# Attention plus gated feed-forward on one core: query weights loaded by halves of 512 columns and 512 rows, and a new order for every engine

## The chip, the cores and the metric

The kernel runs on 1 core of one Trainium2 chip. The metric is the device time of one execution in microseconds (us). Engines are named as in the profile: PE (matmul), PEld (its weight loads), DVE (vector), ACT (activation), POOL, and SP, whose queue issues the DMAs. Stretches of time are counted from the start of the profiled span.

## What is computed

One transformer block on x of 2048 tokens by 1024, in bf16: attention with 32 query heads of width 32 that share one key and one value head, and then a feed-forward layer of width 3584. The reference, cut to what matters:

```python
def _A_ref(x, wq, wk, wv, wo):
    q = (x @ wq).reshape(B, S, H, Dh).transpose(0, 2, 1, 3)
    k = x @ wk
    v = x @ wv
    scores = einsum("bhqd,bkd->bhqk", q, k) * (Dh ** -0.5)
    o = einsum("bhqk,bkd->bhqd", softmax(scores), v)
    return o.transpose(0, 2, 1, 3).reshape(B, S, H * Dh) @ wo

def _B_ref(x, w_gate, w_up, w_down):
    h = sigmoid(x @ w_gate) * (x @ w_up)
    return h @ w_down

h = x + _A_ref(layernorm(x), wq, wk, wv, wo)
out = h + _B_ref(layernorm(h), w_gate, w_up, w_down)
```

## The kernel before

**Tiles.** Tokens are cut into 16 tiles of 128. `mk_xT` (line 628) transposes a normalized tile on PE (tiles 0 to 3; the others go by a DMA transpose, `x_by_dma`, L561), `mk_KV` (line 670) makes keys and values of one or two tiles, `mk_Qc` (line 723) makes the queries of tiles 0 and 1 in four parts of 256 columns, and `mk_Q` (line 739) the other queries, which go through a scratch in DRAM (L752). The normalization of a tile is a chain of small instructions on DVE with one power on POOL (`stats`, L502 to L531; centring L546, scaling L553). POOL copies the key weights four times side by side before `mk_KV` can use them (L483).

**The attention stage** is 512 visits. A visit (`emit_S`, line 858) takes 16 heads of one token tile and one key tile: four S matmuls of 32 rows by 512 that run side by side (S_ps, L601), two exps of 128x1024 on ACT (Pr, L879), and a running sum on DVE (acc, L850). S_ps has three pairs of PSUM banks, so the S matmuls of a visit wait for exps of the visit before. Between visits PE does all other work: PV (probabilities times values, four strips of 32 columns at a time), SUM (row sums, then a reciprocal, L928 or L933), OP (output projection, line 1090), GU (gate and up, line 1218, with a tanh on ACT, L1246, and a product on DVE, L1267) and D (down, line 1301). Their results share two PSUM banks, F_ps; a group may start in a bank when the group before it there has been read out.

**After the last visit** only PE's remaining groups are left: the last PV, SUM and OP, the normalization and transpose of tile 15 (L1119), the rest of GU and D, and the last store.

**What sets the order.** A planner in the kernel (`Plan`) builds one list of instructions for each engine from its own costs and due times (`TUNE`, `KN`). Then each list is put into an order that is written out as a code, and each group gets the bank that a table names:

```python
for e in ORDER:
    lists[e] = reorder(lists[e], ORDER[e])
```

The engines run their lists strictly in that order and wait for each other through semaphores (`emit`, line 1518). `choose_modes` runs a full-width group as four strips of 32 columns (L605 in place of L601) when the stretch before the next visit also holds PV or SUM, so that the array changes its tiling less often.

**The first loads**, as SP issues them: x0, wk, x1, wq0, x2, wv, x3, wq1, x4, wq2, wq3, x5 and so on. wq0 to wq3 are 256 columns each of all 1024 rows:

```python
wq_sb[:, k, :, :],
A_wq[:, k * 256:(k + 1) * 256].rearrange("(a p) n -> p a n", p=P)
```

Of the kernel before, what the change touches and what calls it, by code (L numbers as in the profile page):

```python
# [18 lines left out]
TUNE = dict(bc=0, yld=1, quiet=0, keep=0, ez=1, wvl=2, sa=0, wide=1, pt=1, early=240, look=650, ln_v=1, warm=60, late=300, ws0=1, ws1=0, parts0=4, parts1=4, lord=2, h_ord=2,  # L19
            ho=3, ho2=0, pvl1=1, pvl2=1, col_ok=0, pace0=340, swait=400, parts=12, raw=1, rl=0, nd=2, pc=16,  # L20
            rate=315, pace=250, xd=4, qf=1, dall=1, wo_late=1, nkn=3, few=0, rmin=900, hmin=0, h0=0, h1=250,
            hf=1.2, run=700, sum_few=0, pv_few=4, d_off=0, d_a=0, d_b=0, eb=0, eq=500)


KN = dict(early=120, keep=0, few=4, lag=0, rmin=500, pri=0, sm=1, run=700, hold=100, dg=1, grm=900)
ORDER = dict(
    pe=(
        '0~0B32030=21020A12010~0i32030e72070iq4g20g08120105210201q392090f120102q892090f210209q3j20j01a204030252050242'
        '040252050242040252050242040252050242040252050242043272529103014202410201520501a22702014204034204033202680103'
        '013203034204033203034204033203034203560102034204024204033701a2020102420403420403320302y1f20f0h01320303225802'  # L30
        '014802abndX1l2Yc0201220203s6A142B404015203v8o202010e210202a631624282ihg2030821020o26020s26020gq832030f320301'
        '0u28020h28020362060o2202j2y4D20j0dk2010h027201a305j201020b7207c604e8u2m8w508t20t0g210208a762060202a205220201'
        '0b41125101010512010e12010V12010382320303011201a4024204021201a202a24204021201a204220202041b010311010513011201'
        '05120108120106124801010d220201110101613203010d22020722020321012401a35205030122020461220202051301622202020431'
        '0302120104622202020k12010g1201061242010102120101a203320182019101022202a2033203020122020512010528c1a202051201'
        '0512010522020542040422020j110171013203010212010612010812010512012502011201a104320301031501015132610301a23203'
        '052202230222014801010224015201320304220207220204320151015201012202a201b152c1050201220204320304220135a282c101'
        '0322020361420403220132010233030322020722020432030181083203054204034201720182c1026202044204034202510222015203'
        '110102427104015205226242810182e20102420151926101022101210101420242015182010203b20b0332030472529303b202510201'
        '01320234a27201010332030542026a0201e2010241012272439201420403420402420402513268f2e1h3033203582202010412010532'  # L40
        '03723402710111520103018208720371035101016203215201a2017203a20101040152050452025202a2010501520501c20c52050162'
        '0601820801520264c2a2e2030101625185e20552a273c3i2010263c2920291c2i201010153c2820192d101i2010164d2019101920252'
        '01610163c201810202018208620603620601820837031101320306320303420253020101420403326101610201420334927101012202'
        '01420245b2910191010242130103a202a3f2080204320304520503320302825205013203019102420171030103322154b292d1020152'
        '4172018102a273c1010152025103014202510201520502320303420405420402420402a382d208032202028102220202021201082202'
        '07220221012252017101042202042202a104320161023101032201b1010332030233030385080312010l73520283d1b2e1030528b202'
        '0103a13203034201210102a1420403420102033203033203043203034204327352a203022202024278040124020a81080d2202024103'
        '4222610101a3f14201f103b172040b12010812010d13010382080612010p124501816292010518011201011101021201410401120105'
        '12010615017232030202120105124201010312010f22020812010512010c22020722013101041301042202072201c101a101a15201a2'
        '01b1e101b202010322020241025201210101029252050222020253320303227702a1d203h10203b162c202c101c203020242011253e2'  # L50
        '01060162158101520502520501520344b2820191c101420403520113610152050152050332030532030518010e220208120101110102'
        '12010b410405a30132e101e20201620305a2052202010422114601041601410141030q2501610112c3010332910301011201a1051201'
        '0121010d120102a1031281016103430102320304320304220204320231010322020a51017352a102920203a56206020122a202060312'
        '01061201038232a1030312010512010632030342040542040332030522020542830462a802010242015801c202014404013201620241'
        '920204034204024204a1025205013203044304014204054202a1d10201629301b40405320303320304320305420403320302a482e208'
        '0222020118010655c3a205021282019103420161014104220203a2320303420202924204032202042502032102031801021201052202'
        '02734202810181016101011201052202042801a2010102a1013203042202021242316101042202011352417201110132030632030231'
        '6142030332125601320164c1a2d102a1024211010202b20b028152050132030462060342040242040542040252237501f201017903f5'
        '01j501e203i50102b2e80301k2i201l201k10101c2040102720701625185e20501018207920106016206015232780304340301320304'
        '3203236202010432a4g2e2030581b2920801a262060152010202520512620103054204034204045205024204045295g2e2o301q2l201'  # L60
        'r3030202h30202b103050d82080532030r87080I58i8v503x3020503f501j30105510155019101910203350172020683080283056103'
        '01840571030Z'),
    act=(
        '0a11010411010211010211010211010311010211010~0w12010615010113010b13010711010R11010411010511010911010t11010i11'
        '010g11010k11010711010o11010411010411010b11010711010y13010412010211010711010c12010q12010211010711010311010711'
        '010c11010811010h11010311010611010d11010b11010x11010611010311010l11010r11010q11010a11010611010i11010611010x11'
        '010z11010b12010311010h12010c11010511010511010311010611010s11010i12010j12010311010k11010512010k12010911010311'
        '010311010g'),
    dve=(
        '012251416101680108110121021301311251714161840113615101349171013201713101110101113151210121011241319201025211'  # L70
        '0131011132d16101810141015101f1610101312171115191010141013102215201410231022101032102011101011101051101110104'
        '21020151124131610103110105110111018101b1110141c17101c1910111d10151016101114101110131011101120111010311010115'
        '7361b1a1c10112014102110102110101120101210201310381011201021161310102061g01052111011101011101619101a191029101'
        '11a191b10102011201110101110111010111011501210211310101011131012151010131010101210211010113010131030131011101'
        '11011101011101021101031101190102120103110102110106710421117151410101011101124101012102022102011bd10121010721'
        '0205810411310171320111316101114101012102110121021eg1f10104130101110101a102c10231029101a131020171010232010121'
        '022102021571619181a6011101061101011141215131618101010113010311010321021101210218010411010613010a126132010102'
        '114101110111012102114101021241315c0111010b11010221110103110111010112011201110101113101010315716181a191b1d1c1'
        'e1011101032111010111010181061171310101110101110111011101011101041351416ah1g1i2010321020121012101110113514161'
        '810141310131010111011101011101210211011101021b01053101311101210271011101043111010107110111010111011101033102'  # L80
        '27a191c1b1e2d10105120101110102113121427261a20131011101210131010111310101110106146151719181a1c1b1011201011101'
        '11010211010271b10711410101021101110103110105135141620106210201110103110102124101010d'),
    pool=(
        '04d1h1g102d1c101f301h701n104k201l101le01y90101'),
    sp=(
# [77 lines left out]
MARG = {"sl": 700.0, "rb": 1000.0, "rd": 1200.0, "ha": 900.0, "hT": 200.0, "ql": 1200.0, "xr": 1500.0, "o": 1400.0, "qs": 900.0, "wd": 700.0}  # L163


class Plan:
# [134 lines left out]
def bass_sequential_preLN__grouped_kv_mqa__glu_gated_glu__prompt_kernel(  # L301
# [31 lines left out]
    with ExitStack() as es:  # L333
# [121 lines left out]
        for t in range(2):  # L455
            load_x(t)
# [1139 lines left out]
```

## Time and profile before

| what | value |
|---|---|
| three runs | 1084.05, 1085.04, 1085.25 us (median 1085.04) |
| profiled execution, span from first to last instruction | 1083.9 us, granted PE clock 0.998 |
| instructions | 25911, of them 10588 matmuls |
| busy: PE, ACT, DVE, POOL | 1068.8, 1002.9, 866.3, 36.1 us |
| first S matmul; first exp | 14.42; 14.85 us |
| last S matmul; end of the last exp | 1009.19; 1011.7 us |
| start of the last instruction (DVE, L1314) | 1080.69 us |

The profile names an execution by its span alone; the median of the runs is 1.14 us above it, which is what lies around the span. "Busy" of PE counts a matmul until its modelled end, so that it overlaps with the next one: the time that a matmul takes from the array is the distance from its start to the next start (216 ns for 512 columns), and not the 380 ns of its row. A row of the timeline gives start, duration, engine, line, operation, tile, count, and in brackets the idle time before it with what ended it.

### The profile page before, as it was taken

To read this page: it belongs to the slowest core of one execution; us is meant where nothing else is said; L and a number is where in the kernel's file an instruction comes from. 1 tells how busy PE (TensorE), PEld (TensorE's weight loads), DVE (VectorE), ACT (ScalarE), POOL (GpSimd) and SP (SyncE) were. 2 spreads that over 40 slices of the span, in tenths; PEclk is the share of its full clock that TensorE was granted. 3 is DMA by queue.
4 is the path that set the end of the run, shared out by engine and by line. 5 is a ranking of instruction groups with operands and counts; after the bars stand their busy time and mean duration, and the time that the engine had idled before them with its cause. 6 is when DMAs were issued, how large, how long until landed. Compare 5 with 4: busy or idle time off the path is not lost.

```text
span 1083.9 us, 25911 instructions
## 1 busy us (share of the span) xinstructions
PE 1068.8 (99%) x10588; PEld 432.3 (40%) x10588; DVE 866.3 (80%) x1090; ACT 1002.9 (93%) x1153; POOL 36.1 (3%) x64
## 2 busy tenths in 40 slices
PE   7999999999999999999999999999999999999998
PEld 6533465333333333333333333333333333333343
DVE  8989997887888887896888788888788878888721
ACT  5999999999999999999999999999999999999310
POOL 3300000000000000000000000000000000000000
PEclk9999999999999999999999999999999999999999
DMA  8767797799767796957968685967848796696994
GB/s 248 120 199 219 213 289 222 221 228 249 226 180 222 189 259 162 275 167 202 277 167 226 173 254 162 269 190 195 253 124 257 222 252 165 196 266 150 316 315 125
DMA packets 298935, 234.24 MB, mean 216 GB/s; under 512 B 102080, under 2 KB 285376, under 8 KB 298816
## 3 DMA queue, kind: packets, MB, share of 16 engines
q1 hardware_dynamic: 298816, 232.58, 77.2%
q8 instruction: 84, 1.38, 0.6%
q14 instruction: 35, 0.29, 0.1%
HBM read 203.55 MB, written 8.11 MB: 195 GB/s over the span
## 4 chain that ended last, share of the span: by engine, by line
PE 81%; ACT 15%; DVE 2%; issue 1%; SPq 1%; DMA 1%; DVEq 0%
PE F_ps L601 59%; ACT Pr L879 13%; PE S_ps L601 13%; PE F_ps L605 9%; ACT tnh L1246 1%; DMA ring<-in_A_x_dram 1%; SPq L453 1%; DVE acc L850 0%; DVE rb L928 0%; SPq L462 0%; ACT QTb L879 0%; ACT hnT L879 0%; ACT hact L879 0%; ACT hact L421 0%; DVE h_sb L1314 0%
## 5 line engine op out<-in xcount | busy, mean ns | idle before, releaser
L879 ACT ACTIVATE Pr<-S_ps 128x1024 bf16<-128x1024 f32 x1008 | 944.0, 1077 | 2.3 <-PE S_ps L601 2.0
L850 DVE TENSOR_TENSOR acc<-acc,Pr 128x2048 bf16<-128x2048 bf16 x429 | 522.9, 1220 | 28.7 <-ACT Pr L879 10.3
L601 PE MATMUL F_ps<-ring,hnT 128*128 128x512 bf16 x1312 | 334.5, 380 | 0.9 <-DVE h_sb L1314 0.3
L601 PE MATMUL S_ps<-QTb,kT 32*128 32x512 bf16 x2048 | 208.1, 385 | 2.1 <-ACT Pr L879 1.6
L601 PE MATMUL F_ps<-zone,hact 128*128 128x512 bf16 x732 | 202.2, 380 | 0.0
L601 PEld LDWEIGHTS F_ps<-ring,hnT 128*128 128x128 bf16 x1312 | 115.0, 97 | 155.9 <-issue 45.3
L601 PE MATMUL F_ps<-Pr,Vt 128*32 128x512 bf16 x2016 | 138.6, 382 | 2.3 <-ACT tnh L1246 1.0
L1267 DVE SCALAR_TENSOR_TENSOR act_s<-tnh,F_ps 128x512 bf16<-128x512 f32 x105 | 71.9, 685 | 82.3 <-PE F_ps L601 69.9
L601 PEld LDWEIGHTS S_ps<-QTb,kT 32*128 32x128 bf16 x2048 | 53.4, 91 | 209.4 <-ACT Pr L879 129.3
L1246 ACT ACTIVATE tnh<-F_ps 128x512 f32<-128x512 f32 x112 | 71.5, 639 | 48.0 <-PE F_ps L601 48.0
L601 PEld LDWEIGHTS F_ps<-zone,hact 128*128 128x128 bf16 x732 | 65.7, 98 | 86.8 <-issue 22.9
L605 PE MATMUL F_ps<-ring,hnT 128*32 128x512 bf16 x1104 | 76.6, 380 | 0.1
L601 PEld LDWEIGHTS F_ps<-Pr,Vt 128*32 128x32 bf16 x2016 | 47.1, 96 | 58.5 <-issue 14.6
L601 PE MATMUL F_ps<-zone 128*128 128x512 bf16 (+3 forms) x537 | 65.0, 266 | 2.4 <-DVE rstd L523 0.9
L601 PE MATMUL F_ps<-wo_sb,OT 128*128 128x512 bf16 x243 | 62.9, 380 | 0.2 <-ACT tnh L1246 0.2
L1034 DVE TENSOR_TENSOR oun<-F_ps,oun 128x512 f32<-128x512 f32 x64 | 44.0, 688 | 23.8 <-PE F_ps L601 23.4
L520 POOL TENSOR_TENSOR dsb<-zb,cst 128x1 bf16<-128x1 bf16 x18 | 17.7, 983 | 964.3 <-DVE zb L517 901.5
L605 PE MATMUL F_ps<-zone,hact 128*32 128x512 bf16 x656 | 48.1, 381 | 0.0
L601 PEld LDWEIGHTS F_ps<-zone 128*128 128x128 bf16 x537 | 34.9, 97 | 25.0 <-issue 7.9
L850 DVE TENSOR_TENSOR acc<-Pr 128x2048 bf16<-128x2048 bf16 x31 | 37.2, 1201 | 0.9 <-ACT Pr L879 0.8
L1097 DVE TENSOR_TENSOR h_sb<-F_ps,h_sb 128x512 bf16<-128x512 f32 x32 | 22.1, 691 | 19.6 <-PE F_ps L601 18.8
L605 PEld LDWEIGHTS F_ps<-ring,hnT 128*32 128x32 bf16 x1104 | 26.4, 96 | 27.4 <-issue 10.2
(94 smaller groups left out, 456.1 us busy)
## 6 DMA issues: line engine op xcount, KB each, us to landing
ring<-in_B_w_up_dram SPq DMA_DIRECT2D x312, 256.0 KB, 4.4
ring<-in_B_w_gate_dram SPq DMA_DIRECT2D x310, 256.0 KB, 4.3
rb<-r_scratch SPq DMA_DIRECT2D x120, 64.0 KB, 3.4
zone<-in_B_w_down_dram SPq DMA_DIRECT2D x14, 512.0 KB, 5.2
Pr<-in_B_w_gate_dram SPq DMA_DIRECT2D x18, 256.0 KB, 5.3
ring<-in_A_x_dram SPq DMA_DIRECT2D x16, 256.0 KB, 6.7
h_sb<-in_A_x_dram SPq DMA_DIRECT2D x16, 256.0 KB, 4.4
out_dram<-h_sb SPq DMA_DIRECT2D x32, 128.0 KB, 3.9
```

Of the source, the lines that this page charges most:

```text
L453: x_ld[t] = dma(lambda: SP.dma_start(x_sb(t), xf[t * P:(t + 1) * P, :]), f"x{t}", P * D * 2, prio=0)
L520: g = pl.op("pool", lambda: POOL.tensor_tensor(out=dsb[:, ph, tk], in0=zb[:, ph, tk], in1=half[:, 0:k], op=ALU.pow), [f, c0], prio=0, **sl ...
L601: return lambda: PE.matmul(o, lhsT=l, rhs=r, start=start, stop=stop, **kw)
L605: f.quads = [(lambda j=j: PE.matmul(o[DH * j:DH * (j + 1)], lhsT=l[:, DH * j:DH * (j + 1)], rhs=r, start=start, stop=stop, tile_position=( ...
L850: "dve", lambda lo=lo, hi=hi: DVE.tensor_tensor(out=a[:, lo:hi], in0=src[:, lo:hi], in1=slot[:, lo:hi], op=ALU.add),
L879: exps[u] = pl.op("act", lambda i=i, pb=pb: ACT.activation(out=slot[:, i * 1024:(i + 1) * 1024].rearrange("p (a b) -> p a b", a=2), in_=S_ ...
L1034: oun_ev[(hf, part)] = pl.op("dve", lambda: DVE.tensor_tensor(out=o, in0=F_ps[:, b, :], in1=o, op=ALU.add), [last, oun_ev[(hf, part - 1)]] ...
L1097: h_ev[(t, dc)] = pl.op("dve", lambda: DVE.tensor_tensor(out=h_sb[:, t % NHB, sl], in0=F_ps[:, b, :], in1=h_sb[:, t % NHB, sl], op=ALU.add ...
L1246: box["a"] = pl.op("act", lambda: ACT.activation(out=tnh[:, :], in_=F_ps[:, b, :], func=ACTF.Tanh, scale=0.5), [last, box.get("e")], prio= ...
L1267: e = pl.op("dve", lambda: DVE.scalar_tensor_tensor(out=so, in0=tnh[:, :], scalar=1.0, in1=F_ps[:, b, :], op0=ALU.add, op1=ALU.mult), [las ...
```

## The change

- Query weights: four loads of 512 KB as before, but each is now 512 columns by 512 rows (wq00, wq01, wq10, wq11), so a row of a load is 1024 bytes and not 512. `mk_Qc` waits for the first half (rows 0 to 511), and for the second half only at its fifth matmul.
- The list of first loads is written as `xkqqxvxqq` and then x tiles. The order code for SP, which comes after it, issues x0, x1, wq00, x2, wq01, x3, wk, wv, wq10, wq11, x4.
- `TUNE`, `KN`, `ORDER` and `BANKS` are new. PE has the same groups: 10711 matmuls for 10588, because more groups run as four strips (L605) and fewer at full width.
- `clock`, a second cost table, is walked over the final lists; `emit` sorts the waits of an instruction by the ends that it gives.
- Waits are stated for any order: a buffer's release now names the last matmul of every group that read it, and each D matmul names the transpose that it needs.
- Left out: the constants `third` (three DVE instructions), `pickt` (three POOL instructions) and `mk_BC`, which nothing used.
- ACT takes three more small read-outs (one of QTb, one of hact, one of kT), DVE three fewer.

```diff
-        for t in range(2):
-            load_x(t)
-        wk_ld = dma(...)
-        def load_wq(k):
-                wq_sb[:, k, :, :],
-                A_wq[:, k * 256:(k + 1) * 256].rearrange("(a p) n -> p a n", p=P)), f"wq{k}", D * 256 * 2, prio=0))
...
+        def load_wq():
+            k, h = len(wq_ld) // 2, len(wq_ld) % 2
+                wq_sb[:, k, 4 * h:4 * h + 4, :],
+                A_wq[512 * h:512 * h + 512, k * 512:(k + 1) * 512].rearrange("(a p) n -> p a n", p=P)), f"wq{k}{h}", D * 512, prio=0))
...
+        for c in "xkqqxvxqqxxxxxxxxxxxxx":
...
         def mk_Qc(c, qd):
-                return [(wide(F_ps[:, b, k * P:(k + 1) * P], wq_sb[:, qd, dt, k * P:(k + 1) * P],
-                            xnT[:, 0, dt, c * P:(c + 1) * P], dt == 0, dt == DT - 1), P, "dense", [])
+                return [(wide(F_ps[:, b, k * P:(k + 1) * P], wq_sb[:, qd // 2, dt, (qd % 2) * 256 + k * P:(qd % 2) * 256 + (k + 1) * P],
+                            xnT[:, 0, dt, c * P:(c + 1) * P], dt == 0, dt == DT - 1), P, "dense",
+                         [wq_ld[2 * (qd // 2) + 1]] if dt == 4 else [])
...
-            return Group("Q0" if c == 0 else "Q1", atoms, lambda: [wq_ld[qd], xT_ev.get(c)], after)
+            return Group("Q0" if c == 0 else "Q1", atoms, lambda: [wq_ld[2 * (qd // 2)], xT_ev.get(c)], after)
...
-                         ([hact_ev[(t, ft)]] if dq == 0 else []) + ([wd_ld[ft]] if t == 0 and dq == 0 else []))
+                         [hact_ev[(t, ft)]] + ([wd_ld[ft]] if t == 0 else []))
...
         choose_modes(lists["pe"])
+        clock(lists)
...
-                        want[k] = (d.val, s)
-                for k, (val, s) in want.items():
+                        want[k] = (d.val, s, d.end)
+                for k, (val, s, _) in sorted(want.items(), key=lambda x: x[1][2]):
```

The first matmuls of PE's list show what the new codes do. Before: transposes of x0 (8), Q (16), K and V (8 and 8), transposes of x1 (8), Q (16), 2 more, S of the first visit. After: transposes of x0 (8), Q (32), K (8) and V (8) with 4 of Q among them, S of the first visit, 28 of Q, transposes of x1 (8), S of the second.

More of the change, by code (lines that the diff above doesn't have):

```diff
@@ L16 @@
 SEM = 75.0
[L19 to L25, printed above, removed]
+TUNE = dict(bc=0, yld=1, quiet=0, keep=0, ez=1, wvl=2, sa=0, wide=1, pt=1, early=240, look=650, ln_v=1, warm=60,
+            late=300, ws0=1, ws1=0, parts0=4, parts1=4, lord=2, h_ord=2, ho=3, ho2=0, pvl1=1, pvl2=1, col_ok=0,
+            pace0=340, swait=400, parts=12, raw=1, rl=0, nd=2, pc=16, rate=315, pace=270, xd=4, qf=1, dall=1, wo_late=1,
+            nkn=3, few=0, rmin=900, hmin=0, h0=-300, h1=600, hf=1.0, run=700, sum_few=0, pv_few=4, d_off=0, d_a=0, d_b=0,
+            eb=300, eq=250)
@@ L26 @@
+KN = dict(early=120, keep=0, few=7, lag=0, rmin=500, pri=0, sm=2, run=700, hold=100, dg=1, grm=900)
 ORDER = dict(
     pe=(
[L28 to L41, printed above, removed]
@@ L163, with clock @@
 MARG = {"sl": 700.0, "rb": 1000.0, "rd": 1200.0, "ha": 900.0, "hT": 200.0, "ql": 1200.0, "xr": 1500.0, "o": 1400.0, "qs": 900.0, "wd": 700.0}
+def clock(lists):
+    see = {("act", "dve"): 32, ("act", "pe"): 53, ("act", "sp"): 25, ("dve", "dve"): 34, ("dve", "pe"): 55, ("dve", "pool"): 79,
+           ("dve", "sp"): 27, ("pe", "act"): 37, ("pe", "dve"): 37, ("pe", "sp"): 31, ("pool", "dve"): 34, ("pool", "pe"): 55,
+           ("pool", "pool"): 57, ("sp", "dve"): 24, ("sp", "pe"): 46, ("sp", "pool"): 53, ("sp", "sp"): 17}
+    at = {e: 0 for e in lists}
+    free = {e: 0.0 for e in lists}
+    done, mode, bus = {}, "dense", 0.0
+    while any(at[e] < len(lists[e]) for e in lists):
+        moved = False
+        for e in lists:
+            while at[e] < len(lists[e]):
+                o = lists[e][at[e]]
+                if any(id(d) not in done for d in o.deps + o.order):
+                    break
+                s = max([free[e]] + [done[id(d)] + see.get((d.eng, e), 40) for d in o.deps])
+                if e == "pe":
+                    m = "row" if o.kind in ("S0", "S1") else "col" if o.kind == "col" or len(o.fns) == 4 else "dense"
+                    if m != mode:
+                        s = max(s, free[e] + 102.0)
+                        mode = m
+                    free[e] = s + (7.0 if o.kind == "S0" else max(28.8 if m == "col" else 25.2, o.n / 2.4 + 2.4))
+                    end = s + max(28.0, o.n / 2.4) + 170.0
+                elif e == "sp":
+                    k = o.key.rstrip("0123456789_")
+                    free[e] = s + o.occ
+                    bus = max(bus, s + 1720.0) + o.nbytes * (2.5 if k == "ha" and o.nbytes < 200000 else Plan.SLOW.get(k, 1.1)) / TUNE["rate"]
+                    end = bus + 700.0
+                else:
+                    free[e] = s + o.occ
+                    end = s + o.lat - SEM
+                done[id(o)] = o.end = end
+                at[e] += 1
+                moved = True
+        assert moved, "the order of the engines does not close"
 class Plan:
@@ L761, in after @@
                 return [ev]
[L762 removed]
+            return Group("Q", atoms, lambda: wq_ld[2 * (g // 4):2 * (g // 4) + 2] + [xT_ev.get(k) for k in range(tok // P, (tok + n) // P)], after)
         wd_ld = {}
@@ L921, in sum_gate @@
                 m = kn("sm")
-                return v_done[0] >= NV or m == 2 or m == 1 and pl.pe_mode == "col" or m == 0 and pl.pe_mode == "row"
+                return v_done[0] >= NV or idle > 40 or m == 2 or m == 1 and pl.pe_mode == "col" or m == 0 and pl.pe_mode == "row"
             def after(b, last):
```

235 lines of the change are left out of this document (97 added, 138 removed).

## The prediction

> **What bounds the kernel now.** First the page, then the busy time by stage, then the timeline where a stage loses time. The page:
>
> ```profile
> span 1083.9 us, 25911 instructions
> ...
> PE   7999999999999999999999999999999999999998
> ...
> ACT  5999999999999999999999999999999999999310
> ...
> PE 81%; ACT 15%; DVE 2%; issue 1%; SPq 1%; DMA 1%; DVEq 0%
> ...
> L879 ACT ACTIVATE Pr<-S_ps 128x1024 bf16<-128x1024 f32 x1008 | 944.0, 1077 | 2.3 <-PE S_ps L601 2.0
> ```
>
> Two engines are full, not one. PE is busy in every slice and carries 81% of the chain that ended last; but ACT is as full until the last three slices, and 1008 exps found ACT idle for 2.3 us in all. The windows by stage show where they part (columns: window, length, then busy us of PE, PEld, DVE, ACT, POOL, granted clock, DMA share, GB/s):
>
> ```profile
> 14.40:48.00 33.60, 31.65 (x430) 21.17 (x430) 31.66 (x90) 32.18 (x44) 14.02 (x28) 1.00 0.78 171
> 48.00:150.00 102.00, 101.48 (x1218) 46.41 (x1218) 93.38 (x118) 102.00 (x113) 1.46 (x1) 1.00 0.74 216
> 150.00:171.00 21.00, 18.71 (x243) 11.51 (x236) 16.36 (x17) 19.81 (x24) 0.00 (x0) 0.92 0.93 285
> 171.00:600.00 429.00, 427.58 (x4265) 161.30 (x4263) 353.39 (x410) 428.79 (x491) 8.81 (x8) 1.00 0.79 216
> 600.00:1009.20 409.20, 408.41 (x3974) 151.53 (x3973) 338.78 (x394) 409.09 (x468) 6.73 (x8) 1.00 0.75 209
> 1009.20:1084.00 74.80, 71.20 (x347) 31.42 (x346) 22.78 (x36) 8.48 (x13) 0.55 (x1) 1.00 0.87 247
> ```
>
> From 48 us to the last S matmul at 1009.20, ACT is busy all the time except in 150 to 171. After that only PE matters, for 71.3 us (1009.19 to 1080.5). So the time is: the first visit, ACT's work, ACT's losses, then what PE still has to do.
>
> I add up PE's work in the order of its list with distances between starts read in this trace: 216, 109 and 56 ns for 512, 256 and 128 columns, 25 for fewer, 216 for four strips or four S matmuls together, and 100 for a change of tiling (317 or 312 from an S matmul to a full-width one and back, less 216). Before: 6.9 us up to the first S (warm-up included), 966.5 to the last S, 70.7 after it. The trace took 994.8 for the middle part, so PE lost 28.3 us there (jitter included), and 0.6 after it.
>
> **What the change moves.** The same sums for the new list: 6.6, 971.5 and 66.4. The total rises by 0.3 us (1034 changes of tiling become 1037). 4.9 us of PE's work moves from behind the last visit to before it. That pays only if PE does it in time that it now loses, while ACT is the one that everybody waits for. Part by part:
>
> *1. First visits, DMA.* Before, PE stands still at 17.5 us for wq2, and ACT pays 0.97 us:
>
> ```profile
> 17.51 1.07 PE L601 MATMUL F_ps<-zone 128*128 128x128 bf16 x16 [0.83 <-DMA zone<-in_A_wq_dram]
> ...
> 19.62 1.02 ACT L879 ACTIVATE Pr<-S_ps 128x1024 bf16<-128x1024 f32 x1 [0.97 <-PE S_ps L601]
> ```
>
> After, the query weights stand ahead of x4; with 46 ns for a packet of 1024 bytes in this trace, 86 for 2048 and 11 for 64, sixteen engines bring wq11 by 12.8 us, the slowest of them some 1.5 us later (as they lag here). That wait goes. What is late next is wk, which moves from second to seventh place: packets ahead of it and its own are 4 x 0.69 (x tiles) + 2 x 1.47 (halves) + 0.70 = 6.4 us from the first byte at 2.8: 9.2 us, 10.7 on the slowest engine, for 4.25 now. Then POOL's four copies with the two memsets between them (1.08 + 0.41 + 0.39): 12.6. Keys take 8 x 56 ns, their read-out 0.5: first S at 13.5, for 14.42 now. By the quickest engines it is 12.0; with POOL late, 14.9.
>
> By the Trainium skill (DMA: Bandwidth & Descriptors, Specifications) 512 bytes already reach line rate. The trace disagrees a little: 27 ns for 512 bytes against 46 for 1024, so 512 KB take 1.73 us or 1.47. By the page's rule each half would land 0.26 later, and the sum would be 0.5 higher.
>
> *2. First visits, PE.* The chain of x0 loses its wait for x1, which DVE's order puts in its middle now:
>
> ```profile
> 6.27 0.69 DVE L504 BATCH_NORM_STATS2 st<-ring 128x6 f32<-128x512 bf16 x1 [0.94 <-DMA ring<-in_A_x_dram]
> ...
> 6.88 0.15 DVE L511 CAST mvb<-mv 128x2 bf16<-128x2 f32 x1
> ```
>
> After, the cast follows its input directly; but both statistics of x1 then stand before the scaling of x0, so PE starts at about 8.4 for 9.02. Between the first S and the fifth, the new list has 9.4 us of PE work for 7.7, ACT 7.8 for 7.7. I walked the waits of these rows with the durations above (a read-out of 1024 columns 0.64, of 256 0.3): the later visits start at 16.2, 18.6, 20.3 and 24.6 us, for 16.28, 19.20, 20.97 and 23.34. ACT is then 1.3 us behind, while PE has 1.4 us more done. I take +1.0 for ACT at this point, between -0.9 (fed as early as the first visit) and +2.5 (first S at 14.9).
>
> *3. ACT's work.* 16 small read-outs for 13, at 265 ns each: +0.8; 1.1 of it is in the span that item 2 walked, so -0.3 behind it.
>
> *4. The stretch of 150 to 171 us.* Here PE runs out of work that is ready (visits 68 to 80: 20.1 us of PE work to 23.6 of ACT's), and then the clock falls:
>
> ```profile
> 156.00:163.30 7.30, 5.20 (x67) 3.11 (x68) 5.85 (x7) 7.30 (x10) 0.00 (x0) 1.00 0.92 279
> 163.30:166.80 3.50, 3.50 (x34) 1.89 (x27) 2.94 (x3) 2.97 (x4) 0.00 (x0) 0.51 0.95 298
> ```
>
> At half clock PE is late twice, and ACT loses 0.73 us each time (starts of the exp at 165.45 and the tanh at 168.01, against 904 ns from exp to exp elsewhere). The new list has 21.0 us of PE work to 23.1 of ACT's here, 91% for 85%. I take the drop as gone: -1.5; bounds -1.5 and +1.5 (the same drop, once more).
>
> By the Trainium skill (TensorE: Matmul & The Clock Gate, Part 1) the clock halves after an idle window of about 3.4 us. The trace agrees on the length (3.41 us at half clock) and disagrees on idle: PE was busy for 5.20 of the 7.30 us before. By the page's rule no gap of the new list is long enough, which gives the forecast; by the row a drop can come again, and that is priced in the rivals.
>
> *5. Visits 80 to 511.* ACT's other losses are small (0.37 at 203.45, otherwise 0.2 or less). Of the 28.3 us that PE loses between first and last S, the steadiest stretch (visits 112 to 208: 2.0 us in 185) says that 10 are jitter; the rest is PE waiting for ACT, or for read-outs of F_ps. The new list has more groups that start less than 700 ns of PE work after the one whose bank they take (14 for 6 here; a read-out takes 0.6 to 0.7 and the hand-over 0.25), and its work is less even: in 17 stretches of four visits PE has 4 to 10% more than ACT, in 2 before. I take 0, the value of the present rows, with bounds -2.3 (no losses) and +4.
>
> *6. After the last visit.* 66.4 us of work for 70.7. Four new waits: PV for a tanh (slack 216 ns, so 0.5), GU in the bank that PV just left (slack 0: 0.95), D for a product (slack 448: 0.4), D of tile 15 for the last tanh (slack 0: 0.85): 2.7 us. The chain of tile 15 from OP to the transpose took 7.2 us with two products between its steps and has 3.5 us of PE work to hide it; without those products its rows add up to 4.2, so 0 to 0.9 more, which I leave to the range. 66.4 + 0.6 + 2.7 = 69.7 for 71.3: -1.6; bounds -4.3 and +0.5.
>
> **Sum:** +1.0 - 0.3 - 1.5 + 0 - 1.6 = -2.4 us, on the span of 1083.9: 1081.5; on the median, 1.14 above it: 1082.6 us. The last S then stands at 1008.4, and PE's loss from first to last S at 1008.4 - 13.5 - 971.5 = 23.4 us for 28.3.
>
> **Rivals.** *The order is not what the change says, or the clock falls again.* No half is issued ahead of x1, and wk comes late; with item 2 at its worst (+2.5), or the drop of item 4 back (0 for -1.5), the sum is -0.9: 1084.1. For it: visits 68 to 76 still have 84 to 88% of ACT's work on PE.
> *PE becomes the bound (slower).* If PE's loss between first and last S stays at 28.3 us, with 971.5 us of work from 13.5, the last S is at 1013.3, 4.1 later; with -1.6 behind it the sum is +2.5: 1087.5. It decides above a loss of 25.8 us, where the sum is 0. For it: the uneven work and the tight banks of item 5. Against it: 18 of the 28.3 us are waits, most of them in the first 80 visits, where ACT is full.
> *ACT at its floor.* No losses after visit 80 and no waits behind the last visit: 1008.4 - 2.3, then 67.0: -7.4 in all, 1077.6.
>
> **Numbers.** A measurement of this kernel can tell 0.2%, 2.2 us, from no change. Forecast 0.43 (1079.5 to 1084), first rival 0.25, PE the bound 0.25, ACT's floor 0.07. Faster: 0.36 of the forecast, 0.07 and 0.03 of the others, 0.46; same 0.32; slower 0.22. The range of 1078.5 to 1087.6 leaves out the floor and the worst of the second rival.
>
> **What would show it.** First S near 13.5 and fifth near 24.6; no wait for query weights; no row at half clock near 160; ACT full until a last S at about 1008.4; less than 70 us after it. Wrong if ACT shows idle time before exps in the middle (PE bound), or if PE waits in the tail are longer than the four named.

## Result, and the profile after

| | before | after |
|---|---|---|
| median of the runs, us | 1084.76 | 1095.62 |
| ratio | | 1.0103 (1.0088 to 1.0117) |
| span of the profiled execution, us | 1083.9 | 1095.9 |
| first exp, exp of the fifth visit | 14.85, 23.77 | 16.42, 28.41 |
| exp of visit 80, exp of visit 511 | 170.47, 1009.72 | 175.19, 1022.11 |
| last matmul starts | 1080.27 | 1092.59 |

The change costs 10.9 us where 2.4 were forecast as a gain. Both profiled executions took longer than the median of their kernel: in every run that lists both, the time lies 1.7 to 1.9 us above the span (and not the 1.14 that the forecast used), so the span of 1083.9 stands for some 1085.7 us, and that of 1095.9 for 1097.72. So the stages below add up to +12.0, and the medians to +10.9. The page of the kernel after:

```profile
span 1095.9 us, 26045 instructions
...
PE   7999999999999999999999999999999999999998
...
ACT  4999999999999999999999999999999999999410
...
PE 77%; issue 8%; DVE 6%; ACT 6%; DMA 2%; SPq 0%; POOL 0%; POOLq 0%; DVEq 0%; ACTq 0%
...
L894 ACT ACTIVATE Pr<-S_ps 128x1024 bf16<-128x1024 f32 x1008 | 947.2, 1064 | 4.6 <-PE S_ps L611 3.6
```

The picture by slices is the same: both engines look full. This trace lacks 123 of 10,711 matmul records. The chain's "issue" is not a wait that can be read: 55.6 us of it are one piece near the end (at 985 us), and h1 below, the same lists with every record, shows the same piece. ACT's exps found it idle for 4.6 us instead of 2.3, and that is far from 11: a view by busy time does not show where the time went. The windows by stage (window, length, then busy us of PE, PEld, DVE, ACT, POOL, granted clock, DMA share, GB/s):

```profile
17.20:20.60 3.40, 3.16 (x31) 2.46 (x29) 2.09 (x4) 1.99 (x4) 0.00 (x0) 0.50 1.04 386
14.40:48.00 33.60, 30.53 (x396) 22.11 (x400) 30.09 (x82) 29.62 (x44) 9.45 (x21) 0.95 0.73 174
48.00:150.00 102.00, 98.15 (x1181) 43.35 (x1185) 91.71 (x120) 101.22 (x112) 3.56 (x7) 1.00 0.71 201
150.00:171.00 21.00, 18.94 (x314) 13.36 (x314) 16.87 (x18) 20.69 (x25) 0.00 (x0) 1.00 0.87 272
600.00:1021.60 421.60, 411.56 (x3999) 156.03 (x4048) 344.24 (x400) 419.69 (x477) 8.54 (x7) 1.00 0.79 211
```

The half clock has left 150 to 171 us and stands at 17.20 to 20.60. What separates the kernels is read from the distance between exps of the same visit:

| stage | forecast, us | measured, us |
|---|---|---|
| up to the fifth visit (item 2) | +1.0 | +4.6 |
| from there to visit 80 (items 3, 4) | -1.8 | +0.1 |
| visits 80 to 511 (item 5) | 0 | +7.7 |
| behind the last exp (item 6) | -1.6 | -0.4 |
| sum | -2.4 | +12.0 |

Visits are numbered from 0 to 511, so the fifth is visit 4. Of the -0.4, all but 0.1 stands behind the last matmul: from the exp of visit 511 to the start of the last matmul it is 70.55 us before and 70.48 after.

For the longest stage I use two numbers. ACT's own work from visit 80 to 511 is 825.1 us in every kernel (the distances between starts that the prediction uses); what its time is longer is *ACT's loss*: 14.1 us before, 21.8 after. The same time less PE's work is *PE's loss*: 15.6 and 20.4. So of the 7.7 us, 2.9 are more work for PE and 4.8 are PE waiting. Four executions with the same lists there (after, h1, h2 and t1 below) took 845.9 to 846.9 us for this stage: differences of up to 1 us say nothing.

### The profile page after: what moved, and what is told of

The parts are those of the page before. It is cut to its first block, busy times and chain, and to the rows that moved or that the text cites. A ratio compares the mean times of both kernels' runs of the same rounds, so it can differ in the third digit from the quotient of the medians.

```text
span 1095.9 us, 26045 instructions
## 1 busy us (share of the span) xinstructions
PE 1054.4 (96%) x10588; PEld 435.1 (40%) x10711; DVE 864.8 (79%) x1084; ACT 1009.9 (92%) x1156; POOL 31.7 (3%) x61
## 4 chain that ended last, share of the span: by engine, by line
PE 77%; issue 8%; DVE 6%; ACT 6%; DMA 2%; SPq 0%; POOL 0%; POOLq 0%; DVEq 0%; ACTq 0%
PE F_ps L611 54%; PE S_ps L611 12%; PE F_ps L615 10%; ACT Pr L894 5%; DVE acc L865 3%; DMA hnT<-hn 1%; DMA zone<-in_A_wq_dram 1%; ACT tnh L1225 1%; DVE h_sb L1294 0%; DVE act_s L1247 0%; DVE oun L1009 0%; DVE r_sb L948 0%; DVE hact L444 0%; SPq L474 0%; ACT hact L443 0%
## 5 line engine op out<-in xcount | busy, mean ns | idle before, releaser
L611 PE MATMUL F_ps<-ring,hnT 128*128 128x512 bf16 x1321 | 330.1, 380 | 11.9 <-issue 5.8
L611 PE MATMUL S_ps<-QTb,kT 32*128 32x512 bf16 x2048 | 207.0, 385 | 4.1 <-ACT QTb L894 0.7
L611 PEld LDWEIGHTS F_ps<-ring,hnT 128*128 128x128 bf16 x1387 | 120.2, 97 | 169.2 <-issue 54.2
L611 PE MATMUL F_ps<-zone,hact 128*128 128x512 bf16 x615 | 162.2, 380 | 5.2 <-issue 3.6
L611 PE MATMUL F_ps<-Pr,Vt 128*32 128x512 bf16 x2016 | 135.0, 381 | 1.2 <-ACT tnh L1225 0.6
L611 PEld LDWEIGHTS S_ps<-QTb,kT 32*128 32x128 bf16 x2048 | 53.7, 91 | 202.0 <-ACT Pr L894 131.0
L611 PEld LDWEIGHTS F_ps<-zone,hact 128*128 128x128 bf16 x652 | 57.4, 98 | 77.7 <-issue 20.9
L611 PEld LDWEIGHTS F_ps<-Pr,Vt 128*32 128x32 bf16 x2016 | 47.0, 96 | 57.7 <-issue 14.6
L615 PE MATMUL F_ps<-zone,hact 128*32 128x512 bf16 x976 | 68.6, 381 | 0.0
L611 PE MATMUL F_ps<-zone 128*128 128x32 bf16 (+3 forms) x511 | 59.1, 263 | 5.9 <-DMA zone<-in_A_wq_dram 1.7
L615 PE MATMUL F_ps<-ring,hnT 128*32 128x512 bf16 x852 | 57.6, 381 | 1.6 <-DMA hnT<-hn 0.6
L611 PE MATMUL F_ps<-wo_sb,OT 128*128 128x512 bf16 x225 | 57.1, 380 | 1.1 <-issue 0.6
L611 PEld LDWEIGHTS F_ps<-zone 128*128 128x128 bf16 x522 | 34.8, 98 | 26.1 <-issue 9.1
L1294 DVE SCALAR_TENSOR_TENSOR h_sb<-F_ps,h_sb 128x512 bf16<-128x512 f32 x32 | 22.0, 687 | 21.9 <-PE F_ps L611 18.1
L615 PEld LDWEIGHTS F_ps<-zone,hact 128*32 128x32 bf16 x976 | 21.9, 96 | 25.2 <-issue 10.9
```

The source lines that it names most:

```text
L611: return lambda: PE.matmul(o, lhsT=l, rhs=r, start=start, stop=stop, **kw)
L615: f.quads = [(lambda j=j: PE.matmul(o[DH * j:DH * (j + 1)], lhsT=l[:, DH * j:DH * (j + 1)], rhs=r, start=start, stop=stop, tile_position=( ...
L1294: e = pl.op("dve", lambda: DVE.scalar_tensor_tensor(out=h_sb[:, t % NHB, sl], in0=F_ps[:, b, 0:DW], scalar=0.5, in1=h_sb[:, t % NHB, sl], ...
```

## The experiments

All numbers for visits 80 to 511 from the profiled execution of each, in us; ratios to the kernel before with 95% intervals.

| kernel | PE's work | PE's loss | ACT's loss | ratio |
|---|---|---|---|---|
| before | 823.6 | 15.6 | 14.1 | |
| after | 826.5 | 20.4 | 21.8 | 1.0103 (1.0088 to 1.0117) |
| p0_before_plan_only | 823.2 | 19.6 | 17.7 | 1.0070 (1.0055 to 1.0085) |
| p2_after_plan_only | 826.2 | 19.5 | 20.6 | 1.0119 (1.0098 to 1.0139) |
| h1_kv_loads_first | 826.5 | 19.8 | 21.2 | 1.0098 (1.0083 to 1.0113) |
| h2_kv_group_whole | 826.5 | 20.2 | 21.5 | 1.0123 (1.0108 to 1.0138) |
| w1_before_13_more | 826.4 | 15.3 | 16.6 | 1.0033 (1.0020 to 1.0045) |
| w2_before_49_more | 834.2 | 14.6 | 23.7 | 1.0084 (1.0070 to 1.0097) |
| m1_after_even | 826.5 | 23.1 | 24.4 | 1.0116 (1.0102 to 1.0130) |
| m4_after_dve_order | 826.5 | 20.1 | 21.4 | 1.0085 (1.0071 to 1.0098) |
| c1_before_dve_order | 823.6 | 16.0 | 14.4 | 1.0001 (0.9993 to 1.0010) |
| r1_after_half_readouts | 826.5 | 17.4 | 18.7 | 1.0055 (1.0040 to 1.0070) |
| r2_before_half_readouts | 823.6 | 14.4 | 12.8 | 0.9981 (0.9972 to 0.9991) |
| x1_after_13_less | 823.7 | 23.7 | 22.2 | 1.0108 (1.0091 to 1.0125) |
| x2_half_and_13_less | 823.7 | 18.1 | 16.7 | 1.0047 (1.0033 to 1.0062) |

### The first visits: loads or order

Where PE and ACT stand in the kernel after, by the timeline (start, us, engine, line, what, and in brackets the idle time before and what ended it):

```profile
15.06 0.52 PE L611 MATMUL F_ps<-zone 128*128 128x128 bf16 x9 [1.70 <-DMA zone<-in_A_wq_dram]
15.94 0.40 PE L611 MATMUL S_ps<-QTb,kT 32*128 32x512 bf16 x4 [0.37 <-ACT kT L443]
...
20.15 1.94 ACT L894 ACTIVATE Pr<-S_ps 128x1024 bf16<-128x1024 f32 x2 [1.38 <-PE S_ps L611]
```

The first four matmuls of wq10 stand inside the V part of the first KV group, so keys could be read out only when that half had landed, at 15.01 us; wq11 landed at 16.49. The forecast had 12.8, or 14.3 on the slowest engine. SP's timeline shows what was missed:

```profile
4.57 1.91 SPq L474 DMA_DIRECT2D zone<-in_A_wv_dram  x1
6.53 3.82 SPq L468 DMA_DIRECT2D zone<-in_A_wq_dram  x2
```

An issue normally takes 0.43. Behind wk and wv, each 1024 packets of 64 bytes, that of wv took 1.91 and that of wq10 3.27 of the 3.82: SP stood at it while wk (landed at 10.47) was still to come.

`h1_kv_loads_first`, two loads moved in SP's list:

```diff
             lists[e] = reorder(lists[e], ORDER[e])
+        sp = lists["sp"]
+        for key, at in (("wk", 1), ("wv", 5)):
+            o = next(o for o in sp if o.key == key)
+            sp.remove(o)
+            sp.insert(at, o)
```

> The changed kernel with only two loads moved back in SP's list: wk second and wv sixth, as before the change. Theory C (first visits: wq10 and wq11 land late, at 15.0 and 16.5 us, because SP stood for 1.9 and 3.3 us at the issues of wv and wq10 behind two loads of 64-byte packets): the two halves land 1.5 to 2.5 us earlier, the second exp pair starts at about 18 for 20.15, and the time falls by 1 to 2.5 us, since ACT is the bound until visit 200. Theory D (the losses of the first visits come from the order of PE's list, not from the loads): less than 0.5 us.

`h2_kv_group_whole`, four matmuls moved in PE's list:

```diff
             lists[e] = reorder(lists[e], ORDER[e])
+        pe = lists["pe"]
+        pe[111:122] = pe[115:122] + pe[111:115]
```

> The changed kernel with only four matmuls moved in PE's list: those of wq10 that stood inside the V part of the first KV group now stand behind the first S matmuls. Theory C: PE no longer waits for wq10 (1.70 us before 15.06) ahead of the first S, which starts at 13.9 to 14.2 for 15.94; but the second visit still waits for wq11 (landing at 16.5), so its exp stays at 20.15 within 0.3 us and the time within 0.5 us. Theory D (the order inside the KV group is what costs): the whole 1.9 us arrive at the end.

In h1 the same two halves were issued in 1.53 us together:

```profile
3.31 0.43 SPq L474 DMA_DIRECT2D zone<-in_A_wv_dram  x1
...
6.03 1.53 SPq L468 DMA_DIRECT2D zone<-in_A_wq_dram  x2
```

The halves landed at 12.23 and 13.72, 2.8 us earlier; the second visit's exp came at 16.93 for 20.15 and the fifth visit's at 25.16 for 28.41. The forecast's fifth S, 24.6, plus the 0.43 from S to exp is 25.0. Theory C holds for the landings, and the walk of item 2 was right but for them. In h2 the first exp came at 14.24, 2.2 us earlier, and the second visit's at 20.28, where it was, behind PE's wait for wq11:

```profile
16.11 2.74 PE L611 MATMUL F_ps<-zone 128*128 128x128 bf16 x24 [1.39 <-DMA zone<-in_A_wq_dram]
```

So the wait inside the KV group was not what held the second visit. That the exp stands exactly where it was is in part chance, for in this execution the clock was at half from 15.16 to 21.99; and h2's median is 1.8 us above that of the kernel after, where C allowed 0.5.

h1's profiled execution is 3.8 us shorter than that of the kernel after, its median only 0.9 (C had 1 to 2.5), which the intervals don't separate. Part of the difference is the clock. Rows ahead of a drop (the kernel before, the kernel after) and where none followed (h1, h2; window, length, PE busy, granted clock, DMA share, GB/s):

```profile
159.94:163.35 3.41, 1.83 (x20) 1.00 0.82 218
```

```profile
13.80:17.20 3.40, 1.77 (x29) 1.00 1.03 371
```

```profile
12.00:15.40 3.40, 2.57 (x45) 1.00 1.07 378
```

```profile
1080.12:1083.53 3.41, 1.41 (x8) 1.00 0.49 115
```

In the eight profiled executions with a drop on the way, PE was busy for 0.73 to 1.83 us of the 3.41 us ahead of it. That share alone does not decide, as h2's row shows, and the same lists can go either way: t1 (below) has those of the kernel after up to the last visit, had 1.74 us of PE in 10.0 to 13.4, no drop, and the fifth visit's exp at 26.31 for 28.41. Of these 2.1 us, 1.0 stands ahead of the drop, at the first exp (15.44 for 16.42): wq10 landed at 14.04 in t1 and at 15.01 in the kernel after. From the first exp to the fifth visit's the kernel after took 11.99 us and t1 10.87, so the drop cost 1.1. The loads are worth 1.2 between t1 and h1 (26.31 to 25.16), and 2.1 against the kernel after's execution. By the Trainium skill (TensorE: Matmul & The Clock Gate, Part 1) the activity window is free-running, which fits a drop that comes and goes with the same lists; its "idle window" does not fit, for PE was busy for 21 to 54% of it.

### The middle: fit of the order, or amount of work

`p0_before_plan_only` and `p2_after_plan_only` take the tables away and leave the planner's lists and banks:

```diff
-        for e in ORDER:
-            lists[e] = reorder(lists[e], ORDER[e])
...
-            fb = BANKS[g]
+            fb = b
```

> The kernel before without its tables of order and of banks: the planner's own lists, same loads of 256 columns, same work. Between visits 80 and 511 PE has 823.2 us of work here, 823.6 in the kernel before and 826.5 after the change. Theory A (what the change lost is the fit of the order: PE may issue the S matmuls of a visit only in some 0.3 us, so each stretch that is uneven by one matmul costs ACT about 0.2): a walk of the lists with the durations of the trace and every wait but those for DMAs gives ACT 10.0 us of losses from visit 80 to 511, for 5.7 before and 12.8 after the change, and an end 8.9 us later than before: 1090 to 1096 us. Theory B (PE became the bound because 4.9 us of its work were moved ahead of the last visit): no work was moved here, so no loss there: 1083 to 1087 us, apart from the first visits.

> The changed kernel without its tables of order and of banks: query weights by halves, the planner's own lists, loads in the order x0, wk, wq00, wq01, x1, wv, x2, wq10, wq11. Theory A (fit of the order): the same walk gives an end 3.2 us earlier than the changed kernel with its table, 10.1 us of ACT's losses from visit 80 to 511: 1090 to 1095 us, about that of the kernel before without its tables, so that halves as such cost or bring less than 2 us. Theory B (PE is the bound, 826.2 us of work from visit 80 to 511 as in the changed kernel): within 1.5 us of the changed kernel, 1094 to 1097.

p0 has as much of PE's work as the kernel before and loses 3.6 us more: an order and its banks are worth that much, whatever the loads (theory A; the walk said 4.3). p2 is no better than the kernel after: 1096.69 us where A had 1090 to 1095 and B 1094 to 1097. PE stood still in it for a transposed tile (landed at 53.05), the clock fell to half at 53.29, and ACT paid 3.63 us at one exp:

```profile
53.14 1.79 PE L615 MATMUL F_ps<-zone 128*32 128x256 bf16 x32 [2.68 <-issue]
55.73 1.94 ACT L894 ACTIVATE Pr<-S_ps 128x1024 bf16<-128x1024 f32 x2 [3.63 <-PE S_ps L611]
```

But its middle too lost 20.6, where the walk had promised a gain of 2.7 on the changed kernel: A's figure for it was wrong, and B's was met.

`w1_before_13_more` (and `w2_before_49_more` with 4 for 15):

```diff
         choose_modes(lists["pe"])
+        visit = heads = 0
+        place = collections.Counter()
+        for o in lists["pe"]:
+            visit += o.kind == "S0"
+            place[o.gid] += 1
+            if 80 < visit < 511 and o.n == 512 and len(o.fns) == 1 and o.kind == "wide" and place[o.gid] == 4:
+                heads += 1
+                if heads % 15 == 0:
+                    o.fns = o.fns * 2
```

> The kernel before with 13 matmuls of 512 columns (one in each 15th GU, D or OP group between visits 80 and 511) issued twice, so that these products count one of their eight or more terms doubly; PE has 2.8 us more work there, about as much as the change added (2.9 us), and the order is else unchanged. Theory B (between the visits there is no room on PE, a matmul more arrives at the end): the walk gives 2.7 us more, a time of 1087 to 1088 and ACT's losses from visit 80 to 511 at 16.8 us for 14.1. Theory E (the prediction's: ACT is the bound there and 18 of PE's 28.3 us of losses are room): 0 to 0.8 us.

> The same with 49 matmuls doubled (each fourth group): 10.6 us more of PE's work between visits 80 and 511. Theory B: 9.8 us more by the walk, 1093.5 to 1095.5. Theory E: with 18 us of room at most 3 us more, those doubled matmuls that fall just ahead of S matmuls.

2.8 us of work cost ACT 2.5 us, 10.6 cost 9.6, and the medians rose by 3.3 and 8.2 us. PE's loss stayed at 15.3 and 14.6: the added matmuls filled almost none of it. Theory E, the prediction's own, falls: in the old order a matmul more between the visits is paid nearly in full. (ACT's own work there is as long, 825.1 us for 823.6; whether work added to ACT would be paid too was not tried.)

### Can the new order be mended?

`m1_after_even` is h1 with new codes for PE, ACT and DVE, `m4_after_dve_order` h1 with new codes for DVE alone, `c1_before_dve_order` the kernel before with new codes for DVE and wq2 ahead of x4 (the codes cut to a line):

```diff
     dve=(
...
-        '11010311011101b1021101026121911101710211410112010121020d1101071101110102610181a102910111a1010121013101010311'
...
```

> The changed kernel with wk and wv loaded second and sixth (as in h1_kv_loads_first), and with the order of PE, ACT and DVE between visits 80 and 511 shifted so that the walk of the lists loses less: the same instructions and the same PSUM banks, groups of one bank in the same order, only the places at which groups of the two banks, S matmuls, read-outs and sums interleave. PE's work there stays 826.5 us. Theory A (fit of the order): ACT's losses from visit 80 to 511 fall from 21.2 to 15.0 us (the walk: 12.8 to 6.6) and the time to 1087 to 1090. Theory B alone (the 2.9 us more of PE's work are the price, whatever the order): the losses stay above 14.1 + 2.9 = 17 us and the time above 1090.

> The changed kernel with wk and wv loaded second and sixth (as in h1_kv_loads_first), and with VectorE's list alone shifted between visits 80 and 511, each instruction by a few places at most: read-outs of F_ps ahead of sums of exps where the walk gains by it. PE's and ACT's lists, the banks and the work are those of h1_kv_loads_first. Theory F (part of the middle's loss is PE waiting for read-outs that stand behind sums in VectorE's list; the walk with PE and ACT alone gives 7.3 us of ACT's losses there, with VectorE and GpSimd 12.8): ACT's losses from visit 80 to 511 fall by 3.9 us, from 21.2 to 17.3, and the time to 1090 to 1092. Theory G (only the amount and the order of PE's work count): less than 1 us.

> The kernel before with two shifts: VectorE's list from visit 16 on shifted in the same way, and wq2 loaded ahead of x4. Theory F: 2.0 us less by the walk, and 0.5 to 1 us less at the wait for wq2 at 17.5 us: 1081 to 1083. Theory G: nothing of the first, so 1083.5 to 1084.5.

All three failed: the losses became 24.4, 21.4 and 14.4 where the walk promised 15.0, 17.3 and about 12, and c1 took 1084.88 us where F had 1081 to 1083. In m1 `choose_modes` also ran more groups as four strips (10978 matmuls for 10711). It lost at places that the walk had no price for, by the waits of PE in it (engine, tile, line, awaited: us, times, longest):

```profile
PE F_ps L620 <- DMA ring<-in_B_w_up_dram: 1.8, 3, 0.7
PE F_ps L620 <- DVE acc L874: 1.6, 2, 0.9
PE F_ps L624 <- DMA ring<-in_B_w_up_dram: 1.1, 1, 1.1
```

Matmuls moved forward met gate and up weights that had not landed, and sums of exps that had been put back. So m1 decides nothing between A and B; in m4 and c1 the shifts of VectorE's list brought nothing, so theory F's figures fall, though another order of that list was not tried; and no version that leaves nothing out beats the kernel before.

### The middle: banks

In h1, whose trace has every matmul, PE's longer waits from 171 to 1009 us, and those of the kernel before:

```profile
PE F_ps L611 <- ACT tnh L1225: 0.9, 2, 0.7
PE F_ps L611 <- DMA hnT<-hn: 0.8, 1, 0.8
PE F_ps L615 <- DMA hnT<-hn: 0.6, 1, 0.6
PE F_ps L615 <- DVE h_sb L1294: 0.4, 2, 0.2
PE F_ps L615 <- DVE oun L1009: 0.4, 2, 0.2
```

```profile
PE F_ps L601 <- DVE h_sb L1314: 0.3, 1, 0.3
PE F_ps L601 <- ACT tnh L1246: 0.2, 1, 0.2
```

Shorter waits do not show in this view. From the starts of all matmuls, PE loses 9.1 us at first matmuls of groups in h1 and 5.3 before; 28 of these are over 0.1 us in h1, and 21 of the 28 start 1.06 to 1.43 us after the last matmul of the group that had their bank. So a bank of F_ps changes hands in about 1.25 us from start to start, or 1.03 behind the last matmul's own 0.22. The prediction had 0.95 (0.6 to 0.7 for the read-out and 0.25).

`r1_after_half_readouts` (on h1) and `r2_before_half_readouts`, both without half of the read-outs' columns:

```diff
...
+                    w = 256 if k >= 2 * NST else 512
...
-                        out=so, in0=tnh[:, :], scalar=1.0, in1=F_ps[:, b, :],
+                        out=so[:, 0:w], in0=tnh[:, 0:w], scalar=1.0, in1=F_ps[:, b, 0:w],
```

> The changed kernel with wk and wv loaded second and sixth (h1_kv_loads_first), and with VectorE's read-outs of F_ps (act_s from the fifth slot round on, oun from the fifth half on, both uses of h_sb) over 256 of their 512 columns: half of these results are left out, the lists are the same. Each bank of F_ps comes free some 0.3 us earlier. Theory L (the new order starts more groups just when their bank comes free: in h1_kv_loads_first PE lost 9.1 us at starts of groups between visits 80 and 511, in the kernel before 5.3): ACT's losses there fall from 21.2 to 15 to 17 us (the walk: by 5.2) and the time to 1088 to 1091. Theory K (the loss lies between PE and ACT at the S matmuls, not at the banks): less than 1.5 us.

> The kernel before with the same halves of the read-outs left out. Theory L: ACT's losses from visit 80 to 511 fall from 14.1 to 11 to 12.5 us (the walk: by 2.5), half as much as in r1_after_half_readouts, so that the two orders then differ by little more than the 2.9 us of PE's work that was moved ahead. Theory K: less than 1.5 us, and the two orders stay 7 us apart.

`x1_after_13_less` (on h1) and `x2_half_and_13_less` (on r1) leave out 13 matmuls:

```diff
...
+            if 80 < visit < 511 and o.n == 512 and len(o.fns) == 1 and o.kind == "wide" and place[o.gid] == 4:
+                heads += 1
+                if heads % 6 == 0 and not o.need:
+                    o.fns = []
```

> The changed kernel with wk and wv loaded second and sixth (h1_kv_loads_first), and 13 matmuls of 512 columns left out between visits 80 and 511 (the fourth term of each sixth GU, D or OP group from which nothing waits): 2.8 us less of PE's work, 823.7 us as before the change. Theory B (each matmul there counts in full, as in w1_before_13_more): ACT's losses from visit 80 to 511 fall from 21.2 to 18.7 us. Theory M (in the new order the waits for banks take up the room: the walk gives 1.1 us): 19.5 to 20.5 us.

> The same 13 matmuls left out of r1_after_half_readouts, whose banks come free 0.3 us earlier. Theory B: ACT's losses from visit 80 to 511 fall from 18.7 to 16.2 us. Theory M: once the waits are smaller the work counts in full here too, 16 to 16.5 us, while x1_after_13_less gains only about 1.

Matmuls between visits 80 and 511 that start over 0.1 us later than usual behind the one before them (the median for that pair of shapes), by what ended in the 0.3 us ahead of them; us, and in brackets how many:

| late starts | before | h1 | r2 | r1 | x1 | x2 |
|---|---|---|---|---|---|---|
| behind a read-out of their bank | 3.6 (17) | 5.9 (24) | 1.5 (8) | 3.3 (13) | 6.9 (30) | 3.1 (14) |
| behind the landing of a DMA | 0.4 (2) | 1.7 (2) | 0.2 (1) | 1.0 (2) | 3.6 (4) | 0.8 (4) |
| of S matmuls | 2.4 (7) | 2.5 (10) | 2.9 (8) | 2.8 (11) | 2.9 (12) | 3.7 (17) |

Of the 4.2 us that PE loses more in h1 than before, 2.3 stand at banks and 1.4 at landings. Half read-outs took 2.5 us from ACT's loss in the new order and 1.3 in the old: theory L's direction and ratio, at half its size. But L also had the two orders differ by little more than 2.9 us then; they differ by 5.9 (18.7 and 12.8), for 7.1 before. And half read-outs are less work for VectorE too, so that transposes behind it landed earlier: r1 and r2 do not part the banks from that.

x1 gained nothing: 2.8 us less work, and ACT's loss is 22.2 for 21.2. PE's loss grew from 19.8 to 23.7, at group starts from 9.1 to 12.0. That looks like theory M, but most of the growth is not at banks: landings took 1.9 us more (h1's rows above have no wait for gate weights, and one at L611 for transposes; x1's rows follow), read-outs 1.0.

```profile
PE F_ps L611 <- DMA hnT<-hn: 1.4, 2, 0.9
PE F_ps L611 <- DMA ring<-in_B_w_gate_dram: 0.9, 1, 0.9
```

In x2 the landings did not grow, and the same 13 matmuls are worth 2.0 us in this stage (16.7 for r1's 18.7); the medians differ by 0.7, and the intervals overlap. So the record shows this for the middle: in the old order work on PE is paid nearly in full; banks cost the new order more than the old; and in the new order a matmul less is not simply a gain, because PE then meets weights and transposes that have not landed. With equal work and half read-outs (x2 against r2) 3.9 of the 7.1 us are left, and what they are is open. The landings are the nearest rival; taking those waits away was not tried.

### Behind the last visit

`t1_tail_less_work`, the kernel after without 16 matmuls:

```diff
+        pe = lists["pe"]
+        last = max(i for i, o in enumerate(pe) if o.kind == "S0")
+        end = max(i for i, o in enumerate(pe) if o.tag == "hT")
+        place = collections.Counter()
+        for o in pe[last:end]:
+            place[o.gid] += 1
+            if o.tag == "GU" and place[o.gid] in (3, 4, 5) and not o.need:
+                o.fns = []
```

> The changed kernel with 16 matmuls left out (two or three of the eight or more terms of each GU group between the last S matmul and the last transposes): 3.5 us less of PE's work in the first 20 us behind the last visit. Theory H (these 20 us are set by the chain of the last tile, from its product with V over the output projection and the norm to its transposes, not by PE's work): the last transposes still start 19 to 20 us after the last exp and the end falls by less than 1 us. Theory J (behind the last visit PE's work is what counts): the end falls by 3 us or more, to about 1092.

PE's waits behind the last visit, of the kernel before, the kernel after and t1:

```profile
PE F_ps L601 <- DVE rb L928: 0.2, 1, 0.2
```

```profile
PE F_ps L611 <- ACT tnh L1225: 1.4, 2, 0.9
PE F_ps L611 <- DVE oun L1009: 1.3, 1, 1.3
PE F_ps L1097 <- DVE hn L1081: 0.9, 1, 0.9
```

```profile
PE F_ps L1097 <- DVE hn L1081: 2.2, 1, 2.2
PE F_ps L611 <- DMA hact<-act_s: 1.9, 1, 1.9
PE F_ps L611 <- DVE oun L1009: 1.5, 1, 1.5
```

From the exp of visit 511 to the last matmul, t1 took 69.8 us for 70.5: 3.5 us of work less gave 0.7, because the wait for the norm (L1081) grew by 1.3 and a new one came, for transposed products. Theory H holds for the end; the last transposes did come 1.4 us earlier (18.8 us behind that exp for 20.1). The median, 1097.4, does not help: its four runs spread over 5 us.

## Why the prediction was wrong

*Item 5 is the step that failed: "I take 0, the value of the present rows".* It took PE's 28.3 us of losses as room, since "18 of the 28.3 us are waits", and forecast that they shrink to 23.4. They grew to 34.2 (last S near 1021.6, less 15.94 and 971.5), and ACT's loss in this stage by 7.7 us instead of 0. What the runs showed in its place: in the old order work does not go into that room (2.8 us more cost 2.5, 10.6 cost 9.6: w1, w2), so the 2.9 us that the change put there have to be paid; and PE waits 4.8 us more, in h1 4.2, of which 2.3 are behind read-outs of banks and 1.4 behind landings. The first of these stood in the same item: "14 for 6" groups start with less than 700 ns of PE work behind their bank's last user. At the item's own 0.95 for a hand-over, eight more groups that are short by at least 0.25 us come to 2 us or more; the item gave them no price. The landings it did not mention. That 2.9 us of work cost 2.9 in the new order too is argued and not shown: taking 2.8 out brought 2.0 in x2 and nothing in x1.

*The second rival named the place and the sign, with too small a price.* "PE becomes the bound" gave +2.5 by a loss that stays at 28.3. The last S is 12.4 us later than before, not 4.1: 5.0 more work, 5.9 more loss, and a first S that came 1.5 later.

*Item 2's walk was right, its landing was not.* "Sixteen engines bring wq11 by 12.8 us" counted packets and not the time that SP stands at an issue. (Its "first byte at 2.8" fits the landings as an offset; the first packet of x0 starts at 1.84.) Once wk and wv are issued early (h1), the fifth visit stands within 0.2 us of the forecast. In the change itself the half landed 2.2 us after the forecast's slowest engine, PE stood still, and in the profiled execution the clock fell: the first rival's "the clock falls again", at another place.

*Item 4 was right and worth nothing.* The drop at 163 us is gone, and ACT lost 1.4 us less between visits 76 and 80; but it lost 1.8 us more between the fifth visit and visit 76, and why was not looked into. Nor was the drop a property of the old order: in w2 and c1, with the same PE list up to visit 80, it did not come.

*Item 6 was mis-sized.* 2.7 us of waits were forecast, "0 to 0.9 more, which I leave to the range" for the chain of tile 15; the rows give 3.6, and the gain was 0.4 instead of 1.6. t1 shows why work moved ahead brings little here: those 20 us are set mostly by the chain of the last tile.

So the 4.9 us of work left a stage in which taking it out uncovered the chain of the last tile, for one in which, by w1 and w2, nearly all of it is paid.

## What to carry to other kernels

Idle time of an engine is room only if work can be put there: before pricing added work at nothing, ask what the engine waits for, and test it with a few doubled instructions, as w1 does. Where two banks are all there is, list for each group how long after its bank's last matmul it starts, and compare with the hand-over measured from start to start, not with the read-out's duration. When taking work out of an engine brings nothing, read what it waits for then: in x1 it was mostly loads, and not the banks that were under test. A walk of the lists that leaves out DMA landings ranked given orders roughly (p0), but was not good enough to make better ones (m1, m4, c1).

## What was not expected of the hardware

- The clock fell to half for 3.41 us (6.83 in h2) after 3.41 us in which PE was busy for 0.73 to 1.83 us, never idle all through; the same lists showed it in one execution and not in another, and h2 kept its clock after a window with 1.41 us.
- One DMA issue on SP took 3.27 us (3.71 in h2, 3.10 in t1) behind two loads of 1024 packets of 64 bytes, for 0.43 usually; with those loads issued early the longest before wq11 was 1.58 in h1, 1.69 in x1 and 2.21 in r1, and 2.20 in the kernel before.
- Taking 13 matmuls out of a list of PE made it no faster: PE's loss rose by 3.9 us, 1.9 of it at landings of DMAs.
